# Attention scores on half-height TensorE tiles: one product of 64 rows and 128 columns in place of two of 64 columns

## The chip, the cores and the metric

The kernel runs on one core of one Trainium2 chip. The metric is device time in microseconds (us) of one execution. The engines are TensorE (PE for its products, PEld for its weight loads), VectorE (DVE), ScalarE (ACT), GpSimd (POOL) and SyncE (SP), which here only starts transfers.

## What is computed

Thresholded attention over 8 batches of 8 heads, 576 tokens and 64 values a head, followed by a gated feed-forward layer that mixes over the tokens. Cut to what matters:

```python
scores = q @ k.T / sqrt(64)                      # per batch and head: 576 x 576
thresh = max(scores, axis=-1) - tau
scores = where(scores >= thresh, scores, -1e9)
attn = softmax(scores)                           # over the keys
x = concat_heads(attn @ v)                       # 8 x 576 x 512
h = relu(x @ w_in); u, v = halves(h)             # 512 and 512 wide
v_s = w_spatial @ layer_norm(v) + b_spatial      # over the 576 tokens
out = (u * v_s) @ w_out                          # 8 x 576 x 512
```

All inputs and the output are float32. Queries and keys stay float32 up to the scores. Everything behind the scores runs in 16-bit types.

## The kernel before

**Pairs and steps.** Two heads of a batch make a pair, so there are 32 pairs. Their transposed queries and keys lie together in a tile `qkT` of 128 partitions: partitions 0 to 63 hold the 64 values of the first head, 64 to 127 those of the second. A score product therefore has a contraction of 64 and can use one half (64 rows) of TensorE's array for each head. The 576 queries of a pair are cut in four blocks of 128 and a remainder of 64. A *step* `g` handles one block for both heads. The remainders of two neighbouring pairs share a step. `steps` lists them: an even pair has steps `c` = 0 to 3, an odd one 4, 0, 1, 2, 3. That makes 144 steps: 128 with 128 queries of one pair (`c < 4`) and 16 shared ones (`c == 4`).

**Scores of a step.** `part(g, h, lo, hi)` multiplies the queries of the step with keys `lo` to `hi` of head `h` into a buffer in PSUM, TensorE's result memory. In the kernel before it does so in two products for every step. Each takes 64 queries (`k` = 0 and 1) as weights, so it occupies 64 rows and 64 columns of the array, a quarter, and writes partitions 0 to 63 or 64 to 127 of the buffer (`halves[k]`). The profile shows each float32 product as two passes, each a weight load and a matmul. `scores(g)` issues three parts: 160 keys of head 0, 416 of head 1, 416 of head 0. `scores_end(g)` issues the last, 160 keys of head 1. A step then is 4 parts of 2 products of 2 passes: 16 weight loads and 16 matmuls.

The cuts at 160 and 416 follow the banks of PSUM (512 numbers to a partition). Head 0's scores start at column 96 and head 1's at 864, so that the 160 keys of either head fall in the middle bank. The last part may write that bank only after head 0's 160 have left TensorE. This is kept by a wait: `opened[g]` is the last product of the first part. `turn_bank` lets another engine (mostly GpSimd) execute an empty instruction that waits for it, and the first product of the last part waits for that (`follow`). `s_ring` has two buffers, so step `g + 2` may start only when ScalarE has read the scores of step `g`.

**Behind the scores.** VectorE takes the negative maximum over the keys (`top`, line 850) and adds the threshold (`shift`, line 856). ScalarE reads the scores twice, once for each head (`spread`, lines 871 and 874), and for most steps once more from SBUF (`exps`, line 909). Some steps are masked by VectorE (`keep` and `pick`) instead. DMA transposes the numerators (`turn_p`, line 914), and TensorE multiplies them with `v` (`weigh`, lines 491 and 496, on the full array). TensorE also makes the transposes of queries and keys in float32 (`qk_main`, line 434, and `qk_rem`, line 453) and the products of the feed-forward layer (lines 642, 709, 738 and 767), all on the full array of 128 by 128. Some products at lines 504, 510, 627 and 630 use 128 rows by 64 columns.

**Order.** Everything is issued in an order written out by hand: the strings `ORDER`, one for each batch, and `LAST`. In them `S` is `scores`, `G` `turn_bank`, `Y` `scores_end`, `M` `top`, `E` and `F` `spread`, `P` the products with `v`. Every engine executes its own instructions in this order, and between two steps there is almost always other work for TensorE.

Of the kernel before, what the change touches and what calls it, by code (L numbers as in the profile page):

```python
# [184 lines left out]
def kernel(  # L185
# [18 lines left out]
    B, H, S, D = q.shape  # L204
# [5 lines left out]
    P = 128  # L210
# [15 lines left out]
    s_ring = [ps_s.tile([P, 1536], F32, name=f"s{i}") for i in range(2)]  # L226
# [147 lines left out]
    def shape_bias(_):  # L374


        for n in range(3):
            part = wsb[:, :, S + n]
            nc.gpsimd.tensor_copy(out=part, in_=bias)
            if n < 2:  # L380
                nc.gpsimd.tensor_tensor(out=bias, in0=bias, in1=part, op=ALU.subtract)
# [17 lines left out]
    qks, xns, xts = {}, {}, {}  # L399
# [86 lines left out]
    halves = [slice(64 * k, 64 * k + 64) for k in range(2)]  # L486
# [303 lines left out]
    at = (96, 864)  # L790
# [16 lines left out]
    cut = 512 - at[0]  # L807
    opened, turned = {}, {}

    def part(g, h, lo, hi):  # L810

        i, c = steps[g]
        made = []
        for k in range(2):
            n, m = (i, 64 + c * P + 64 * k) if c < 4 else (i - 1 + k, S)
            made.append(nc.tensor.matmul(  # L816
                out=s_ring[g % 2][halves[k], at[h] + lo:at[h] + hi],
                lhsT=qks[n][halves[h], 0, m:m + 64],
                rhs=qks[n][halves[h], 1, 64 * (1 - h) + lo:64 * (1 - h) + hi],
                start=True, stop=True))  # L820
        return made

    def scores(g):

        opened[g] = part(g, 0, cut, S)[1]
        part(g, 1, S - cut, S)
        part(g, 0, 0, cut)

# [266 lines left out]
    def run_token(tok, it):  # L1095
# [19 lines left out]
        m = 2 * b + a[0] if a else 0  # L1115
        if kind in "SGYMHKEFBZWCAT":
            {"S": scores, "G": lambda g: turn_bank(g, relay), "Y": scores_end, "M": top, "E": lambda g: spread(g, 0),
             "F": lambda g: spread(g, 1), "H": lambda g: top(g, slice(0, 1)),
             "K": lambda g: top(g, slice(1, 2)), "B": shift, "Z": exps, "W": mask, "C": keep, "A": pick, "T": turn_p}[kind](g)
# [124 lines left out]
```

## Time and profile before

| what | value |
|---|---|
| median of 3 runs | 437.4 us (435.09 to 437.69) |
| the profiled execution, its own time | 435.42 us |
| its span, first to last instruction | 433.6 us |
| granted TensorE clock, mean | 1.000 |
| first and last score product start | 6.2 and 396.0 us |
| VectorE, maximum over the keys (line 850) | 144 x 1362 ns = 196.1 us |
| ScalarE, reading the scores (lines 871 and 874) | 288 x about 745 ns = 199.9 us |
| ScalarE, last exponent (line 909) | 96 x 1173 ns = 111.6 us |

In a line of the profile's groups, `64*64` is the part of the array that a product occupies, rows by columns. `64x160 f32` is the moving operand, partitions by elements. Behind the first bar stand the busy time and the mean duration of one in ns, behind the second the idle time of the engine before them and what ended most of it. Matmuls are pipelined: a record runs from the acceptance of the matmul to the modelled end of its last result, so records overlap.

### The profile page before, as it was taken

What the parts mean: (1) busy time and instruction counts of PE and PEld (TensorE: products, weight loads), DVE (VectorE), ACT (ScalarE), POOL (GpSimd) and SP (SyncE); (2) the same over time, 40 slices, a digit from 0 to 9 for tenths busy, and PEclk for the clock granted to TensorE, in tenths of its full rate; (3) what the DMA queues carried; (4) which work ended last, traced back from release to release, by engine and by line L of the source; (5) the groups of instructions that cost most, each with busy time, mean ns of one, the idle gap of its engine ahead of it and who ended that gap; (6) DMA issues with size and microseconds to landing.
All of it is one profiled execution on the core that took longest, in us unless ns stands there. A gap on an engine that the chain in (4) does not pass through costs nothing.

```text
span 433.6 us, 12917 instructions
## 1 busy us (share of the span) xinstructions
PE 407.3 (94%) x5028; PEld 253.7 (58%) x5028; DVE 374.6 (86%) x681; ACT 383.9 (89%) x587; POOL 167.5 (39%) x374
## 2 busy tenths in 40 slices
PE   7678879989999999998999999999999999999995
PEld 4446655565755666574665656555666656564642
DVE  6999989898989889987889988988999999998652
ACT  4999989999999988998988999999999989999262
POOL 1253525682335611545143713356114630264020
PEclk9999999999999999999999999999999999999999
DMA  7999999999899998999979999999999999889923
GB/s 195 224 237 232 246 247 221 194 212 197 226 241 212 246 208 183 218 184 178 254 139 250 216 159 248 233 209 205 232 209 232 181 232 194 172 124 193 164 68 118
DMA packets 224700, 88.15 MB, mean 203 GB/s; under 512 B 195648, under 2 KB 220352, under 8 KB 224640
## 3 DMA queue, kind: packets, MB, share of 16 engines
q1 hardware_dynamic: 224192, 86.75, 99.7%
q8 instruction: 39, 0.64, 0.6%
q10 hardware_dynamic: 368, 0.33, 0.2%
q0 software_dynamic: 80, 0.26, 0.2%
q14 instruction: 21, 0.17, 0.2%
HBM read 32.79 MB, written 9.44 MB: 97 GB/s over the span
## 4 chain that ended last, share of the span: by engine, by line
PE 64%; ACT 13%; DVE 8%; DMA 6%; issue 4%; POOL 3%; SPq 0%; ACTq 0%; DVEq 0%; POOLq 0%
PE s L816 26%; ACT e L874 6%; PE f L738 6%; DVE s L850 5%; PE f L496 5%; PE f L709 5%; PE f L434 4%; PE f L642 4%; PE f L767 4%; DMA pT<-p 3%; ACT p L909 2%; DMA xT<-xn 2%; ACT e L871 2%; PE f L491 2%; PE f L627 1%
## 5 line engine op out<-in xcount | busy, mean ns | idle before, releaser
L850 DVE TENSOR_REDUCE s<-s 128x2 f32<-128x1152 f32 x144 | 196.1, 1362 | 21.3 <-PE s L816 18.0
L816 PE MATMUL s<-qkT 64*64 64x160 f32 (+1 forms) x2304 | 171.4, 415 | 12.6 <-ACT e L874 6.6
L816 PEld LDWEIGHTS s<-qkT 64*64 64x64 f32 x2304 | 106.5, 131 | 71.3 <-ACT e L874 18.8
L874 ACT ACTIVATE e<-s,negm 128x576 f32<-128x576 f32 x192 | 133.1, 744 | 9.6 <-DVE negm L856 7.0
L909 ACT ACTIVATE p<-e 128x1152 f16<-128x1152 f32 x96 | 111.6, 1173 | 0.7 <-PE s L816 0.2
L871 ACT ACTIVATE e<-s,negm 128x576 f16<-128x576 f32 x96 | 66.8, 746 | 5.0 <-DVE negm L856 2.9
L320 POOL CAST v<-vl 128x512 bf16<-128x512 f32 x32 | 20.2, 631 | 77.0 <-PE s L816 65.7
L496 PE MATMUL f<-v,pT 128*128 128x65 bf16 x984 | 44.4, 194 | 0.0
L496 PEld LDWEIGHTS <-pT 128*128 128x128 f16 x1024 | 41.8, 98 | 2.2 <-issue 0.2
L293 POOL COPY qn<-ql 128x512 f32<-128x512 f32 x31 | 20.4, 659 | 49.9 <-PE s L816 47.5
L902 DVE TENSOR_TENSOR p<-e 128x576 int32<-128x576 int32 x48 | 37.2, 778 | 0.4 <-PE s L816 0.2
L738 PE MATMUL f<-wsT,vn 128*128 128x512 bf16 x135 | 33.0, 380 | 0.0
L491 PE MATMUL f<-v,pT 128*128 128x130 bf16 x123 | 27.3, 222 | 3.6 <-DMA pT<-p 3.5
L709 PE MATMUL f<-xT,w_in 128*128 128x512 bf16 x116 | 29.7, 380 | 0.5 <-ACT qkT L414 0.3
L694 POOL TENSOR_SCALAR vn<-vrel,rs,nm 128x512 bf16<-128x512 f32 (+1 forms) x35 | 28.1, 801 | 3.6
L642 PE MATMUL f<-w_in,xT 128*128 128x512 bf16 x112 | 27.9, 380 | 0.3 <-DMA xT<-xn 0.3
L446 POOL COPY qkT<-qkT 64x64 f32<-64x64 f32 x32 | 9.5, 296 | 44.8 <-PE s L816 17.6
L534 DVE TENSOR_TENSOR xn<-f,r 128x384 bf16<-128x384 f32 x46 | 24.9, 551 | 1.3 <-PE s L816 0.8
L856 DVE TENSOR_SCALAR negm<-s 128x2 f32<-128x2 f32 x144 | 22.2, 154 | 4.0 <-PE s L816 1.5
L767 PE MATMUL f<-w_o,gT 128*128 128x512 bf16 x100 | 25.4, 379 | 0.1
L893 DVE TENSOR_SCALAR e<-e 128x1152 uint16<-128x1152 f16 x48 | 23.0, 478 | 0.1
L687 POOL TENSOR_TENSOR rs<-rs,mhalf 128x1 f32<-128x1 f32 (+1 forms) x35 | 21.2, 607 | 2.9
(171 smaller groups left out, 531.4 us busy)
## 6 DMA issues: line engine op xcount, KB each, us to landing
vl<-in_v_dram SPq DMA_DIRECT2D x16, 512.0 KB, 5.3
ql<-in_q_dram SPq DMA_DIRECT2D x15, 512.0 KB, 4.6
kl<-in_k_dram SPq DMA_DIRECT2D x15, 512.0 KB, 5.3
out_dram<-oo SPq DMA_DIRECT2D x12, 512.0 KB, 3.7
pT<-p SPq DMA_TRANSPOSE x141, 4.6
uT<-in_moe_w_in_dram SPq DMA_DIRECT2D x3, 512.0 KB, 5.1
uT<-in_moe_w_spatial_dram SPq DMA_DIRECT2D x2, 576.0 KB, 4.4
vx<-in_v_dram SPq DMA_DIRECT2D x16, 64.0 KB, 4.3
```

Source lines behind the costliest of these rows:

```text
L491: nc.tensor.matmul(out=t[:, at:at + 130], lhsT=pt[:, 4, rows], rhs=vt[:, 4:6, :].rearrange("p b d -> p (b d)"), start=True, stop=False)
L496: nc.tensor.matmul(out=t[:, at + 65 * h:at + 65 * h + 65], lhsT=pt[:, 5 * h + j, rows], rhs=vt[:, 6 * h + j, :], start=False, stop=(h == 1 ...
L642: nc.tensor.matmul(out=t, lhsT=x_of(b, f, slice(c * P, (c + 1) * P)), rhs=w_in[:, f, 512:1024], start=(f == 0), stop=(f == 3))
L709: nc.tensor.matmul(out=t, lhsT=w_in[:, m, f * P:(f + 1) * P], rhs=x_of(b, m, slice(0, 512)), start=(m == 0), stop=(m == 3))
L738: nc.tensor.matmul(out=t, lhsT=vn[:, c, f * P:(f + 1) * P], rhs=wsT[:, c, 0:512], start=(c == 0), stop=(c == 4))
L767: nc.tensor.matmul(out=t[:n], lhsT=gs[b][:, f, c * P:c * P + n], rhs=w_o[:, f, :], start=(f == 0), stop=(f == 3))
L816: made.append(nc.tensor.matmul(out=s_ring[g % 2][halves[k], at[h] + lo:at[h] + hi], lhsT=qks[n][halves[h], 0, m:m + 64], rhs=qks[n][halves ...
L850: nc.vector.tensor_reduce(out=nm[:, heads], in_=view(s_ring[g % 2], at[h0], dims), axis=AX.X, op=ALU.max, negate=True)
L871: nc.scalar.activation(out=half_e(g)[0][:, S * h:S * h + S], in_=s, func=ACT.Exp, bias=bias_, scale=scale if steps[g][1] == 4 else 1.0)
L874: nc.scalar.activation(out=e, in_=s, func=ACT.Prelu, bias=bias_, scale=scale if steps[g][1] == 4 else 1.0, alpha=1e30)
L902: nc.vector.tensor_tensor(out=numerators(g).bitcast(I32), in0=e.bitcast(I32), in1=kept.bitcast(I32), op=ALU.bitwise_and)
L909: nc.scalar.activation(out=numerators(g), in_=e_ring[g % 3].rearrange("p h s -> p (h s)"), func=ACT.Exp)
```

## The change

A step with `c < 4` now makes each part as one product with all 128 queries of the block as weights: 64 rows and 128 columns of the array, written to all 128 partitions of the buffer. Steps with `c == 4` keep two products, since their two groups of 64 queries come from two pairs. `opened[g]` is now the last of the products made, be it one or two. The issued order, the keys of each part, the buffers and the waits are the same.

```diff
         made = []
-        for k in range(2):
-            n, m = (i, 64 + c * P + 64 * k) if c < 4 else (i - 1 + k, S)
+        for k in range(1 if c < 4 else 2):
+            n, m = (i, 64 + c * P) if c < 4 else (i - 1 + k, S)
             made.append(nc.tensor.matmul(
-                out=s_ring[g % 2][halves[k], at[h] + lo:at[h] + hi],
-                lhsT=qks[n][halves[h], 0, m:m + 64],
+                out=s_ring[g % 2][slice(0, P) if c < 4 else halves[k], at[h] + lo:at[h] + hi],
+                lhsT=qks[n][halves[h], 0, m:m + (P if c < 4 else 64)],
                 rhs=qks[n][halves[h], 1, 64 * (1 - h) + lo:64 * (1 - h) + hi],
                 start=True, stop=True))
         return made
 
     def scores(g):
 
-        opened[g] = part(g, 0, cut, S)[1]
+        opened[g] = part(g, 0, cut, S)[-1]
```

## The prediction

> **What bounds the kernel now.** I began with the page: busy time of each engine, then the engines' shares of the chain that ended last.
>
> ```profile
> PE 407.3 (94%) x5028; PEld 253.7 (58%) x5028; DVE 374.6 (86%) x681; ACT 383.9 (89%) x587; POOL 167.5 (39%) x374
> ...
> PE 64%; ACT 13%; DVE 8%; DMA 6%; issue 4%; POOL 3%; SPq 0%; ACTq 0%; DVEq 0%; POOLq 0%
> ```
>
> TensorE is busiest and holds 64% of the chain, but ScalarE at 89% and VectorE at 86% are close. A longer step on TensorE is therefore felt almost fully, while a shorter one soon meets the other two. The same list by line gives the score products (line 816) 25.6% of the span, 111 us.
>
> Next, all instructions of that line. The figures behind "x2304:" are the shortest, the median and the longest in ns. Below them stand its two forms from the groups by form, with the mean in ns.
>
> ```profile
> L816 PEld LDWEIGHTS s<-qkT x2304: 129/133/133, 6.2 to 395.9; 64*64 64x64 f32 x192
> L816 PE MATMUL s<-qkT x2304: 296/428/561, 6.2 to 396.0; 64*64 64x160 f32 x144, 64*64 64x416 f32 x48
> ```
>
> ```profile
> L816 PE MATMUL s<-qkT 64*64 64x416 f32 x1152 | 167.8, 521 | 0.0
> L816 PE MATMUL s<-qkT 64*64 64x160 f32 x1152 | 132.1, 308 | 12.6 <-ACT e L874 6.6 <-ACT e L871 3.9 <-DVE negm L856 1.5
> ```
>
> In the single records a matmul of 160 keys lasts 296 ns and one of 416 keys 509, except in the first pass of each head in a step, where they last 347 and 560. Then (3 x 296 + 347) / 4 = 309 and (3 x 509 + 560) / 4 = 522, the means above. Three numbers follow. A key costs (509 - 296) / 256 = 0.83 ns a pass, so 160 keys stream in 133 ns and 416 in 346. What remains of a record, 296 - 133 = 163 ns, is the way of the last result out. And 347 - 296 = 51 ns is a weight load of 64 float32 columns that nothing covers.
>
> Third, the chain of waits in a stretch where TensorE sets the pace (start, duration, what, number of instructions):
>
> ```profile
> 202.22 1.13 PE s L816 x12
> 203.35 1.19 PE f L738 x5
> 204.54 0.44 PE f L434 x4
> 204.97 1.13 PE s L816 x12
> 206.10 0.26 PE f L453
> 206.36 1.08 PE f L738 x5
> ```
>
> A step, from the start of its first record to the end of its last, takes 1201 ns in nearly all 144 cases. It adds 1.13 us to the chain, since its first load starts 70 ns before the record of the matmul ahead of it ends. The five products of line 738 take 1.08 us behind others on the full array but 1.19 behind a step. So each change of the array's division costs something on the way in and on the way out.
>
> **What a step is made of.** In the records of one step, the four quarters of the array (head 0 and 1, queries 0 to 63 and 64 to 127) accept their first pass 7, 14 and 20 ns after each other and then stream side by side. Each head streams 2 x 133 + 2 x 346 = 958 ns. With the exposed load of 51, the way out of 163 and the last quarter's 20 ns this is 1192 of the 1201; the rest is 2 or 3 ns between passes.
>
> **The change, part by part.** *Streaming:* each head still sends 576 keys twice through its 64 rows, so the 958 ns stay, provided the two heads still run side by side. The two halves of the queries already ran side by side, so merging them removes no streaming. The way out stays at 163: matmuls on the full array show 273 - 0.83 x 128 = 167 (line 434).
>
> *Instructions:* 128 steps x 8 = 1024 matmuls and as many loads go, 5028 to 4004 each. That saves only staggering: head 1 is accepted about 7 ns behind head 0, and no quarter follows it. The gain lies between 6 and 13 ns a step; I take 10.
>
> *Weight load:* this decides. The first load of a step is exposed, because nothing of the step can run before it, and the matmuls ahead are on another division of the array. It grows from 64 to 128 columns. No record shows 64 rows by 128 columns. The nearest rows are the step's own load, 51 ns for 64 columns, thus 102 for 128 at the same rate, and the float32 transposes on the full array, here in one stretch:
>
> ```profile
> L434 PEld LDWEIGHTS f<-identf,qn x4: 140/141/144, 208.5 to 208.8; 128*128 128x128 f32 x4
> L434 PE MATMUL f<-identf,qn x4: 272/273/332, 208.5 to 208.9; 128*128 128x128 f32 x4
> ```
>
> There 128 columns expose 332 - 273 = 59 ns. So the load is between 59 and 102 ns, and the step gains 8 to 51. I take 102: same line, same kind of product. A transpose takes one pass where a score product takes two, so its load may well be another one. Moreover, where the two loads of the halves are 36 ns apart (the step at 120.98 us), both still last 129 ns; had they shared one path, the first would have been shorter.
>
> The Trainium skill ("TensorE: Matmul & The Clock Gate", section "LDWEIGHTS (loading the stationary operand)") gives a load as columns divided by 1.2 ns, 53 ns for 64 and 107 for 128. The score products' 51 fits it and the transposes' 59 does not; by it the step would gain 54 ns ahead of the staggering. It is a rule against the change.
>
> The other loads of a step are covered: each is issued as the matmul before it on its half starts, and the shortest cover is a pass of 133 ns against 102. One more comes late: that of the last part, which waits for the empty instruction. In 128 of the 144 steps it starts 131 ns or more ahead of its matmul, still enough, since both ends move with the step. In 16, where the wait is an instruction of its own, the lead is 57 to 70 ns. There 102 ns would make the last part about 36 ns late; 14 steps with `c < 4` x 36 = 0.5 us.
>
> *Changes of division:* a first load starts 70 ns before the end of the record ahead, against 163 ns between products of one division: 93 ns lost going in, and as much coming out. The records show this for 64 by 64 and for 128 by 64, not for 64 by 128. I keep it at nothing gained; the other end is both losses and the exposed loads gone, priced under the second rival.
>
> The Trainium skill ("TensorEngine Tiling (Array Packing)", section "Key Properties") says that changing the tiling mode, not just the tile, drains TensorE, and lists 64 by 128 as a mode of its own. No run so far shows it for that one; by it no drain goes and the sum stands.
>
> *Elsewhere:* no transfer, buffer or wait changes. VectorE's maximum and ScalarE's reads begin later by what the step grows.
>
> *Sum:* 51 - 10 = +41 ns a step. If every step counts, 128 x 41 ns + 0.5 = +5.7 us. The least is what stands on the chain: 111 us / 1.13 = 98 steps, of which 128/144, 87, are changed: 87 x 41 ns = +3.6 us. I take the middle, +4.7: the span goes from 433.6 to 438.3 and the profiled execution from 435.4 to 440.1. That execution was 2.0 us under the median of the runs, 437.4, from which I forecast 442.1 us.
>
> **Rivals.** *The load costs what the transposes' costs* (+8 ns): with the staggering a step changes by -2 ns and with the ends of it by -5 to +2, times 87 to 128 steps at most 0.6 us: 437. The price speaks for it, the spread loads against it.
>
> *The division by rows alone needs no drain*, and this ends faster. On the way in, 93 ns and the 51 of the load would vanish, on the way out up to 110 (1.19 against 1.08), 254 ns less a step. 87 steps would give 22 us, were nothing else in the way. But between 20 and 400 us ScalarE is busy 356.9 of 380 us, which leaves 23 us with no wait at all, and it waits for VectorE too. I take half, 11: 426. If only the load is drawn ahead and hidden, -61 ns x 87 = -5 us: 432. It decides as soon as the first matmul of a step shows no more than 296 ns. Against it: every change of division in the trace shows the 93 ns. For it: the one kind that would be used is the one not shown.
>
> *The two heads lose their concurrency at the load*, each waiting for the other's: head 1 starts another 102 ns later, +143 a step, times 87 to 128 steps is 12 to 18 us: 452. Streaming one after the other would cost 0.96 us more a step, 123 us: 560. Against both: today the heads' loads start 13 ns apart and both first passes show the same 51 ns.
>
> **How the numbers follow.** Chances: forecast 0.58, load like a transpose 0.20, no drain (either form) 0.11, heads one after the other 0.11. A measurement of this kernel can tell about 1%, 4.4 us, from no change. The forecast's +3.6 to +5.7 lies across that, 0.36 of its 0.58 above. Slower: 0.36 + 0.11 = 0.47, and 0.01 of the second case: 0.48. Faster: 0.11. Within 1%: 0.41. The forecast's own range is 439.5 to 444.5, its ends and 1.3 us for the spread of the runs. For 8 in 10 the range takes in the load like a transpose, with the same spread, down to 435, and above it 446.5, where the loads of the last part are late in more steps; outside lie the other two cases.
>
> **What would show it.** Right: matmuls of the form 64*128, first passes of 398 and 611 ns, later ones still 296 and 509, steps of 1.24 us, 4004 matmuls, line 738 still at 1.19 us behind a step. A first pass near 355 shows the transposes' price, one at 296 the missing drain. A step near 1.35 us shows heads that wait for each other, one over 2 us heads that stream in turn. The forecast is wrong in its last step if steps grow by 41 ns and the span by less than 3.6 us; then the chain had other work as late as TensorE's.

## The result and the profile after

| | before | changed |
|---|---|---|
| median of 21 runs each | 435.71 us (432.44 to 437.69) | 438.54 us (436.85 to 440.39) |
| ratio, 95% interval | | 1.0064 (1.0044 to 1.0083) |
| profiled execution, its own time and span | 435.42 and 433.6 us | 437.67 and 435.6 us |

The change costs 0.64% of 435.7, that is 2.8 us (1.9 to 3.6). The forecast was +4.7 us.

The page of the changed kernel: busy time of each engine, then the engines' shares of the chain.

```profile
PE 410.7 (94%) x3962; PEld 276.4 (63%) x4004; DVE 374.4 (86%) x681; ACT 385.0 (88%) x587; POOL 167.6 (38%) x374
...
PE 70%; ACT 13%; DVE 9%; DMA 4%; issue 3%; DVEq 0%; ACTq 0%; SPq 0%
```

There are 4004 weight loads, as counted. Of the matmuls, 42 records are missing, so TensorE's busy time is somewhat too small here. TensorE's share of the chain rose from 64% to 70%, DMA's fell from 6% to 4%, and GpSimd's 3% are gone from it. DMA's loss is the first sign of what the forecast missed.

The instructions of one step of the changed kernel (count, then shortest, median and longest in ns):

```profile
L816 PEld LDWEIGHTS s<-qkT x8: 183/186/188, 204.3 to 205.1; 64*128 64x128 f32 x8
L816 PE MATMUL s<-qkT x8: 296/455/614, 204.3 to 205.2; 64*128 64x160 f32 x4, 64*128 64x416 f32 x4
```

The first passes last 401 and 614 ns, the later ones 296 and 509. So a load of 64 rows by 128 columns exposes 105 ns where 64 columns expose 51. Both heads show it and are accepted 7 ns apart: they still load and stream side by side. A step takes 1242 ns, 41 more than before. The chain of the same stretch, now from a step on:

```profile
204.34 1.17 PE s L816 x6
205.51 0.26 PE f L453
205.77 1.08 PE f L738 x5
206.85 1.17 PE s L816 x6
```

A step adds 1.17 us where it added 1.13. No other of these links changed: the five products of line 738 behind others still take 1.08.

### The profile page after: what moved, and what is told of

Its sections match the earlier page's. It is cut to its first block, busy times and chain, and to the rows that moved or that the text cites. A ratio compares the mean times of both kernels' runs of the same rounds, so it can differ in the third digit from the quotient of the medians.

```text
span 435.6 us, 10827 instructions
## 1 busy us (share of the span) xinstructions
PE 410.7 (94%) x3962; PEld 276.4 (63%) x4004; DVE 374.4 (86%) x681; ACT 385.0 (88%) x587; POOL 167.6 (38%) x374
## 4 chain that ended last, share of the span: by engine, by line
PE 70%; ACT 13%; DVE 9%; DMA 4%; issue 3%; DVEq 0%; ACTq 0%; SPq 0%
PE s L816 28%; DVE s L850 6%; PE f L738 6%; PE f L496 5%; ACT e L874 5%; PE f L434 5%; PE f L709 5%; PE f L642 4%; PE f L767 4%; ACT p L909 3%; ACT e L871 2%; PE f L491 2%; DMA pT<-p 2%; PE f L627 2%; DMA uT<-in_moe_w_spatial_dram 1%
## 5 line engine op out<-in xcount | busy, mean ns | idle before, releaser
L816 PE MATMUL s<-qkT 64*128 64x160 f32 (+3 forms) x1280 | 177.3, 426 | 13.1 <-ACT e L874 7.3
L816 PEld LDWEIGHTS s<-qkT 64*128 64x128 f32 (+1 forms) x1280 | 128.9, 175 | 61.7 <-ACT e L874 18.3
L738 PEld LDWEIGHTS <-vn 128*128 128x128 bf16 x140 | 12.6, 98 | 15.1 <-issue 2.5
```

The lines of the kernel that those rows point to most:

```text
L738: nc.tensor.matmul(out=t, lhsT=vn[:, c, f * P:(f + 1) * P], rhs=wsT[:, c, 0:512], start=(c == 0), stop=(c == 4))
L816: made.append(nc.tensor.matmul(out=s_ring[g % 2][slice(0, P) if c < 4 else halves[k], at[h] + lo:at[h] + hi], lhsT=qks[n][halves[h], 0, m: ...
```

## Where the time went

I compared the starts of all 144 steps in two records of the changed kernel and three of the kernel before (two of them from the runs 12 and 13 below). The 143 distances from step to step, mean of the changed kernel's less mean of the kernel before:

```
89 distances that grew by 25 to 60 ns, 39.5 on average     +3.52 us
four shared steps with a step right behind (pairs)         +0.63
behind step 22                                             -1.38
behind step 71                                             -0.77
behind step 80                                             +0.63
steps 4-6, 17-19, 23, 24 (in part half the clock, below)   -0.06
all others                                                 -0.17
sum                                                        +2.40
```

The first row is the mechanism of the forecast, in number (87 steps were forecast) and in size (41 ns). The second and the third are fixed: they stand in every record. The rows of steps 71 and 80 are waits for transfers. That of step 71 differs from record to record in the kernel before too. That of step 80 stands, among these five records, in the changed kernel's two alone, at two sizes.

**Behind step 22** TensorE waits in the kernel before. Its products there, from the timeline (start, duration, line, and in brackets the idle time ahead of it):

```profile
57.77 0.22 PE L491 MATMUL f<-v,pT 128*128 128x130 bf16 x1
57.82 0.41 PE L496 MATMUL f<-v,pT 128*128 128x65 bf16 x8
60.16 0.23 PE L491 MATMUL f<-v,pT 128*128 128x130 bf16 x1 [1.93 <-DMA pT<-p]
```

The chain of that record passes through the transfer itself, not through what TensorE did meanwhile:

```profile
55.16 4.95 DMA pT<-p
60.12 0.05 issue
60.16 0.23 PE f L491
```

In the changed kernel the same products follow each other without a wait (the first three lines):

```profile
58.44 0.22 PE L491 MATMUL f<-v,pT 128*128 128x130 bf16 x1
58.49 0.42 PE L496 MATMUL f<-v,pT 128*128 128x65 bf16 x8
58.75 0.22 PE L491 MATMUL f<-v,pT 128*128 128x130 bf16 x1
58.80 0.41 PE L496 MATMUL f<-v,pT 128*128 128x65 bf16 x8
59.90 1.24 PE L816 MATMUL s<-qkT 64*128 64x160 f32 x8 [0.69 <-ACT e L874]
```

TensorE comes 0.7 us later there, and the transpose lands 2.2 us earlier, at 57.87 in place of 60.12. It was issued 0.5 us earlier and took 3.2 us in place of 5.0. What is left is a shorter wait, for ScalarE: TensorE is idle for 0.69 us ahead of step 23 (the last line). So of the wait of 1.93 us not all is gained.

**Behind step 80** the opposite happens. In the chain of the changed kernel a transfer of `xT` stands ahead of two products of line 642:

```profile
218.60 4.69 DMA xT<-xn
223.29 0.05 issue
223.33 0.60 PE f L642 x2
```

TensorE waits 0.83 us for it. In the first record of the kernel before, this transfer took 2.90 us and landed at 221.96, and the products that read it start at 222.56 without a wait.

**A pair.** Where a shared step (64 by 64) is directly followed by a step of the same pair, before and in the changed kernel:

```profile
158.67 2.17 PE L816 MATMUL s<-qkT 64*64 64x160 f32 x32
```

```profile
158.89 2.37 PE L816 MATMUL s<-qkT 64*64 64x160 f32 x24
```

Before, the second step started 0.77 us after the first and ran into its gaps, since both used the same division of the array. Now it starts 1.13 us after it, and the pair takes 0.20 us more. There are four such pairs, at steps 58, 112, 121 and 130.

## The experiments

Two theories stood against each other. **A:** a step costs what was forecast, but delays of TensorE are taken up in part where it waits for transposes by DMA. **B:** delays arrive nearly whole, and the change pays some 1.9 us back because it issues 1024 products and loads fewer. Ratios are to the kernel before, measured beside each run.

**1 to 3: longer steps without, and with, the change.** Head 1's first part gets more keys. They repeat keys of the pair, into columns that nobody reads, so only TensorE's time grows. The first two edit the kernel before, the third the changed one.

```diff
-        part(g, 1, S - cut, S)
+        part(g, 1, S - cut, S + (26 if steps[g][1] < 4 else 0))    # second run: 64
```

> The kernel before with 26 more keys in head 1's first part of each step of 128 queries (columns nobody reads): 26 x 2 passes x 0.83 ns = 43 ns more a step, about what the change added (41 ns), with all its products of 64 columns kept. Steps of 1.24 us. Theory A (a part of every delay of TensorE is taken up where it waits for transposes by DMA, so about 0.54 of 128 x the step's growth arrives): +2.9 us, ratio 1.007. Theory B (a delay arrives nearly whole, and the change pays about 1.9 us back by 1024 fewer products and loads): +4.9 us, ratio 1.011.

> The same with 64 more keys: 106 ns more a step, 13.6 us if all arrived. Theory A with a fixed share of 0.54: +7.3 us, ratio 1.017. Theory A with a fixed amount that is taken up once (about 2 us): +10.3 us, ratio 1.024. Theory B: +12.1 us, ratio 1.028.

> The changed kernel with the same 26 more keys: steps of 1.285 us, 5.5 us more in steps than the changed kernel. Theory A with a fixed share: 2.9 us over the changed kernel, ratio 1.013 to before. Theory B, or A with the slack used up already: 4.9 us over the changed kernel, ratio 1.018.

| run | step | ratio (95%) | us |
|---|---|---|---|
| before + 26 keys | +43 ns | 1.0049 (1.0029 to 1.0070) | +2.1 |
| before + 64 keys | +106 ns | 1.0180 (1.0150 to 1.0209) | +7.8 |
| changed + 26 keys | +41 + 43 ns | 1.0157 (1.0123 to 1.0192) | +6.8 |

43 ns a step in the kernel before, with all its products kept, cost as little as the change: theory B's 1.011 lies outside. The second run fits a constant share (7.3 us) and neither a fixed amount of 2 us (10.3) nor theory B (12.1). The third lies between the two expectations (5.7 and 7.7) and decides nothing. In the record of the second run step 23 follows step 22 after 2.82 us, without the wait for the transpose. In that of the first the distance is 4.18 us, with it.

**4 and 11: the changed kernel with shorter steps.** The first try left out 26 keys of head 1 in 112 steps (their columns keep old values).

```diff
-        part(g, 1, S - cut, S)
+        part(g, 1, S - cut, S + (-26 if steps[g][1] < 4 and g >= 18 else 0))
-        part(g, 0, 0, cut)
+        part(g, 0, 26 if steps[g][1] < 4 and g >= 18 else 0, cut)    # run 11 alone
```

> The changed kernel leaving out 26 keys of head 1 (old values stand in their columns) in the 112 steps of 128 queries from step 18 on: those steps are back at 1.20 us, with the 1024 products fewer kept. Theory A: +0.2 us over before, ratio 1.000 (its steps before 18 keep their growth). Theory B: faster than before by about 1.5 us, ratio 0.9965.

It gave 1.0085 (1.0052 to 1.0118), which neither theory had. The run was ill made: head 0 streams as long as head 1, so the steps stayed longer than meant (1.24 us in its record), and it says nothing of either. With both heads shortened:

> The changed kernel leaving out 26 keys of each head in the 112 steps of 128 queries from step 18 on (the run with head 1 alone could not shorten a step, as head 0 streams as long). Steps of 1.20 us with 1024 products fewer. Theory A: what is left is the growth before step 18 (0.5 us) and the four pairs (1.0 to 1.4 us), partly taken up: +0.5 to +1.9 us, ratio 1.001 to 1.004. Theory B (fewer products and loads pay 1.9 us back): -0.4 us or less, ratio 0.999 or lower.

Measured 1.0028 (1.0001 to 1.0055), as theory A has it. With steps of the old length the changed kernel is not faster than the one before, so the 1024 products and loads fewer pay nothing back that these runs can see.

**5 and 6: no wait for the transposed numerators.** Both kernels, with the products with `v` reading a constant. The transposes are still made.

```diff
-                weigh(hold["t"], 130 * k, pT_ring[g % 12], v_ring[i % 4])
+                weigh(hold["t"], 130 * k, pT_const, v_ring[i % 4])
```

> The kernel before with the products with v reading a constant in place of the transposed numerators (the transposes are still made): TensorE no longer waits for them. The base for the next run; 0 to 4 us faster than before.

> The changed kernel with the same edit. Theory A: with that wait gone in both, the change costs 4.3 to 5.3 us, ratio of this run over the last 1.010 to 1.012. Theory B: still 2.8 us, 1.0065.

Ratios 0.9989 (0.9958 to 1.0020) and 1.0104 (1.0074 to 1.0134), medians 434.81 and 439.27 us: now the change costs 4.5 us. By the means of the runs it is 5.0 us (3.6 to 6.4, two standard errors to either side).

**8 and 9: no transposes of numerators at all.** As above, and the 141 transfers are not made either.

> The kernel before without the 141 transposes of numerators by DMA at all; the products with v read a constant. Most small transfers and with them most waits for transfers should go. Base for the next run; 2 to 6 us faster than before.

> The changed kernel with the same edit. Theory A (waits for transfers take up a part of the growth): without them the change costs what its records show, 3.3 to 3.6 us of longer steps and 1.0 to 1.4 where a step follows a shared one directly, together 4.3 to 5.0 us over the last run, 1.010 to 1.012. If transfers have no part in it: 2.8 us, 1.0065.

Ratios 0.9956 (0.9929 to 0.9984) and 1.0071 (1.0046 to 1.0095), medians 433.52 and 438.60 us: 5.1 us, and 5.4 by the means (4.4 to 6.3). The mean load of the DMA engines between 20 and 400 us fell from 1.06 to 0.37 by the table of windows, so these two are apart from the transposes' traffic. In their records step 23 follows step 22 after 2.89 and 2.93 us: the difference of 1.3 is gone. In the second, a wait of 1.0 us for `xT`, behind step 80, is left, which its base does not have. Run 6 has it too (0.85 us).

By its two ratios each pair of runs says 1.0115. At the far ends of the intervals this is 1.005 to 1.018 and 1.006 to 1.017, which still touches the 1.0064 of the change, but counts the spread of the kernel before twice. Run against run, both intervals above leave out the change's 2.8 us. This speaks for theory A: the change costs more where the numerators' transposes are not waited for. The records add up to it: from run 5 to 6 and from run 8 to 9 the longer steps make 3.8 and 3.7 us, the pairs 0.6, and the wait for `xT` makes the distance behind step 80 longer by 1.1 and 1.2.

**10: the four pairs.** The step behind a shared one again in products of 64 columns.

```diff
-        for k in range(1 if c < 4 else 2):
-            n, m = (i, 64 + c * P) if c < 4 else (i - 1 + k, S)
+        whole = c < 4 and g not in (59, 113, 122, 131)
+        for k in range(1 if whole else 2):
+            n, m = (i, 64 + c * P + 64 * k) if c < 4 else (i - 1 + k, S)
```

> The changed kernel with the four steps that follow a shared step directly (59, 113, 122, 131) in products of 64 columns again, so that no change of division stands between the two. Their pairs should start 0.77 us apart again in place of 1.13, together 1.4 us, of which 1.0 is on the way of what follows: 0.5 to 1.4 us faster than the changed kernel, ratio to before 1.003 to 1.005. If those four pairs do not matter: 1.0064.

Measured 1.0027 (1.0008 to 1.0046), and the pair is back at its old length:

```profile
158.49 2.17 PE L817 MATMUL s<-qkT 64*64 64x160 f32 x32
```

The cost of the pairs is real. The records give 0.6 us for it, less than the 1.0 to 1.4 expected, because the step behind gives back half of what the start lost. The ratio gained 1.6 us, with about 1.2 to either side, and so can't fix the size. Nor need all of it be the pairs': the record of this run has no wait behind step 80 (2.90 us), which the changed kernel's have.

**7: halves first.** Only the first two parts of a step in products of 64 columns, the other two in 128.

```diff
-        opened[g] = part(g, 0, cut, S)[-1]
-        part(g, 1, S - cut, S)
+        opened[g] = part(g, 0, cut, S, True)[-1]      # True: two products of 64 columns
+        part(g, 1, S - cut, S, True)
```

> The changed kernel with only the first two parts of a step (head 0's 160 keys, head 1's 416) in two products of 64 columns again, the other two in one of 128. If the load of a step's start is the whole cost, and going from 64 by 64 to 64 by 128 inside a step is free, first passes are 347 and 560 ns again, steps 1.20 us and the time is that of before. If that change of division drains TensorE too, a step is 0.1 us or more longer than the changed kernel's and the ratio over 1.02.

500.7 and 511.7 us. The second expectation holds, and far beyond its size. A step from its record:

```profile
202.09 1.82 PE L817 MATMUL s<-qkT 64*64 64x160 f32 x12
```

It takes 1.82 us, 0.58 more than in the changed kernel; 128 x 0.58 = 74 us. The record is that of the run of 511.7 us, in which TensorE had half the clock from 18.6 to 52.7 us (0.50 in the table of windows), well ahead of this step. The other run, of 500.7, is 62 us above the changed kernel. The first passes are 347 and 560 ns again. But head 0's 128-column load is at 202.95, although its half of the array streamed its last key at about 202.41: it waited for head 1's 64-column products as well, the last of which ends at 203.02. So this change of division drained both halves of the array, and the load of 105 ns is exposed behind it.

**12 to 14: further records of the same kernels.**

> The kernel before, unchanged, for a second record. The first had TensorE waiting for transposed numerators behind steps 22 (1.9 us) and 71 (1.6 us), the changed kernel's only behind 71. If that wait belongs to the kernel before, it stands there again with more than 1.3 us behind 22, and step 23 starts 4.2 us or more after step 22; if it comes and goes with the transfers of an execution, step 23 follows after 2.9 us as in the changed kernel, and a wait of some us may stand elsewhere.

> A third record of the kernel before, unchanged: the distances of steps 22 and 23 and of 71 and 72 as in the run before it, 4.2 and 4.9 us where the waits belong to the kernel, 2.9 and 3.5 us where they come and go.

> The changed kernel, unchanged, for a second record. Its growth outside of waits (steps 41 ns longer, four pairs 0.37 us) must repeat to 0.1 us; its waits for transfers need not.

| record | 22 to 23 | 71 to 72 | 80 to 81 |
|---|---|---|---|
| before, three | 4.26, 4.31, 4.32 us | 4.93, 4.25, 3.18 | 2.86, 2.86, 2.86 |
| changed, two | 2.92, 2.92 | 3.47, 3.22 | 3.69, 3.30 |
| changed with edits (runs 3, 4, 10, 11) | 2.89, 2.92, 2.92, 2.92 | 3.48, 3.82, 3.75, 4.18 | 2.95, 3.15, 2.90, 3.70 |

The wait behind step 22 belongs to the kernel before. It is in all three records, and in none of the changed kernel's. The wait behind 71 comes and goes. That behind 80 is in no record of the kernel before and in both of the changed kernel, but runs 3 and 10 do not have it. The changed kernel's 39.5 ns a step and its four pairs repeat to 0.1 us.

## Why the prediction was wrong

**The step was right, term by term.** The load measured 105 ns against 102 taken and grew by 54 against 51, half as many products saved 13 ns of staggering (20 to 7) against 10, streaming was as counted, and the two heads stayed side by side. The drains stayed: a step's first load still starts about 72 ns before the record ahead ends. A step grew by 41 ns against 41, where the two differences of 3 ns cancel by luck. What spoke against the transposes' price (59 ns), the spread of the loads, spoke rightly. The Trainium skill's figure ("TensorE: Matmul & The Clock Gate", section "LDWEIGHTS (loading the stationary operand)"), 53 and 107 ns, is within 2 ns of both measured loads. Its other rule ("TensorEngine Tiling (Array Packing)", section "Key Properties"), that a change of tiling mode drains, holds for 64 by 128 too: the 72 ns and run 7 show it.

**What failed is the last step, from the step to the whole: "The least is what stands on the chain", 3.6 us, and the middle of 3.6 to 5.7 above it.** The growth on TensorE's own distances, 3.5 us, was that least almost exactly. But a chain of one record is a lower bound only while its other links keep their length. One of them, 4.95 us of DMA at step 22, did not. Its length is a transfer's and does not follow TensorE's. In the changed kernel TensorE comes later, the transfer lands earlier, and the distance is 1.4 us shorter. So 3.5 + 0.6 - 1.4 = 2.7 us, near the 2.8 measured. That it comes so near is partly luck: the shorter wait behind 71 (-0.8) and the new one behind 80 (+0.6) nearly cancel in these records. The prediction named the case ("then the chain had other work as late as TensorE's") and gave it no price, though the chain's 6% of DMA was in its first view.

**A second cost was overlooked, and it hid part of the first miss.** "No transfer, buffer or wait changes" was true of what is issued, but not of how long transfers take and are waited for (steps 22 and 80). And four steps stand directly behind a shared one. Before, they shared its division; now a drain lies between them, +0.6 us. It was to be read from the order: `S13` and `S14`, or `S4` and `S5`, with no other work of TensorE between.

**The price for late last parts (0.5 us) was nothing.** The forecast set the load of 102 ns against a lead of 57 to 70. That was the lead of the second product's load, which comes 36 ns behind the first and which the change takes away. The first load of the last part has a lead of 87 to 100 ns in these 16 steps of the kernel before. In the changed kernel it has 96 to 109, and its matmul starts 810 to 812 ns after the step's first load, as in nearly all other steps.

**The level.** The forecast of 442.1 us also started from a median of three runs, 437.4, where 21 give 435.7.

**Open.** That the wait behind step 22 is gone is shown, and so is that the change costs 4.5 to 5.4 us where such waits are taken out. Why the transpose lands so much sooner is not: its queue was ahead by half a microsecond and its transfer 1.7 us shorter, and no run separates the two. The shorter transfer is no chance of one record: it took 4.2 to 5.0 us in the three records of the kernel before, and 3.2 or 3.3 in the two of the changed kernel and in runs 3, 4, 10 and 11. Nor are the fewer products needed for it: with them all kept it took 3.3 us in run 2, but 4.5 in run 1. Why the transfer of `xT` behind step 80 takes longer in the changed kernel is open too. Run 1, the kernel before with 43 ns more a step and the wait behind step 22 kept, cost no more than the change; in its record the wait behind step 71 was short (3.22 us, 0.9 less than the mean of the three), and one record can't say whether that is its own.

No version that computes the whole was faster than the kernel before. The best of the changed ones is run 10.

## What to carry to other kernels

When a product is split over more of the array's columns, count the weight load that nothing covers, not the products: here half as many instructions did the same streaming and left a first load twice as long. To turn such a sum into a change of the whole, split the chain into links that follow the engine and links that transfers set, and take the second kind as able to shrink or grow. Keep neighbouring work on one division of TensorE, and look for such neighbours in the order before changing the shape of one of them.

## What had not been expected of the hardware

A change from 64 by 64 to 64 by 128 inside a step cost 0.58 us, since one half of the array waited for the other to drain. And in two of the three records of the kernel before, and in run 1's, the wait behind step 22 is followed by half the clock for 3.4 us. In the table of windows of run 12's record, 56 to 64 us, the last three figures are granted clock, DMA share and GB/s; inside the stretch, from 60.8 to 64.1 us, the clock is 0.50:

```profile
56.00:64.00 8.00, 6.24 (x95) 4.49 (x94) 5.51 (x11) 5.65 (x9) 1.21 (x3) 0.80 1.09 226
```

The wait is that of the first line below. Step 23, 1.20 us elsewhere in the kernel before, is 2.20 there:

```profile
59.63 0.23 PE L491 MATMUL f<-v,pT 128*128 128x130 bf16 x1 [1.57 <-DMA pT<-p]
61.17 2.20 PE L816 MATMUL s<-qkT 64*64 64x160 f32 x16
```

By it, step 24 starts 0.7 us later and step 25 1.0. So more than a wait of 1.6 us itself was lost there. That the wait is the cause is not shown: in the first record the same wait, of 1.93 us, had no such sequel.
